# A convolution layer's Fourier transforms: the taps' spectra in a stage of their own, a fixed order on three engines, and the stream's first radix-2 stage on TensorE

## The chip, the cores and the metric

The kernel runs on one core of one Trainium2 chip. Its time is the device time of one execution, in microseconds (us). It is one launch: two state-space convolution layers and two attention layers, one after the other (called a, b, c and d here: a and c are the convolutions).

## The reference

The stream `x` has 2048 rows (time) and 640 columns (channels). Each layer is normalised, run, and added to the stream. This is the convolution layer, the only part that the change touches:

```python
P = jnp.exp(logdA[:, :, None] * l[None, None, :])
K = jnp.einsum("dn,dnl,dn->dl", Cc, P, dB).real          # 2048 taps for each of 640 channels
...
Kf = rfft2(pad(K, L))                                    # spectrum of the taps, length 4096
Uf = rfft2(pad(u^T, L))                                  # spectrum of the stream
y  = irfft2(Uf * Kf)[..., :L]^T + u * Dskip
...
x = x + _A_ref(_layernorm(x), ...)                       # layer a, and again as layer c, same taps
x = x + _B_ref(_layernorm(x), ...)                       # layers b and d: 32-head attention
```

All of it is float32. The taps are the same in layers a and c.

## The kernel before

The taps `K` are built first (`kgen`) and stored in device memory as `kd`. The convolutions then work on five chunks of 128 channels (`NCH = 5`, `DC = 128`). A transform of length 4096 is split in two: a dense part on TensorE (matrix products with a table of cosines and sines, `wf` forward, `wi` inverse, 4 MB each) and an FFT of length 8 on VectorE (`fft8`: 2 instructions of 1024 elements for each partition, 14 of 512).

For one chunk `c` of the stream:

- ScalarE writes the normalised stream to `xn`, 16 instructions of 128x128 (L615).
- `fwd`: TensorE makes four tiles `z` of 1024 columns in PSUM (L522). A `z` holds two halves, and the stage after it is a radix-2 butterfly over them: ScalarE copies one half to `zs` (L525), VectorE writes sum and difference into the spectrum `A` (L527, eight instructions of 512 elements for a chunk). Then `fft8` forward (L93 to L115).
- VectorE multiplies `A` by the spectrum of the taps `kh`, a complex product: six instructions of 2048 elements (L630 to L635). Then two more of 2048 (L636, L637), and `fft8` in the other direction, again L93 to L115.
- TensorE makes four tiles `y` with the table `wi` (L648), and VectorE adds each to the stream (L652, "the residual").

In layer a the spectrum `kh` of each chunk is made on the way, by the same `fwd` from `kd` (tiles `zk`, `Ak`; `Dskip` is added to the first tap at L601), and stored to device memory, 2 MB for a chunk (L603). Layer c loads it (L595). So layer a makes ten forward transforms and layer c five. In the last two chunks VectorE also takes the statistics for the next layer's normalisation (L557, L559), and in the last one it splits the attention's weights (L671).

The order on TensorE, VectorE and ScalarE in these layers is set by a scheduler that knows priorities and buffers, not by the source. It runs parts of one chunk's `fwd` between parts of another chunk's product and inverse.

Of the kernel before, what the change touches and what calls it, by code (L numbers as in the profile page):

```python
# [11 lines left out]
F32 = mybir.dt.float32  # L12
# [3 lines left out]
AF = mybir.ActivationFunctionType  # L16
ALU = mybir.AluOpType
# [66 lines left out]

def fft8(nc, A, B, R, sg):

    ADD, SUB = ALU.add, ALU.subtract  # L90
    plus, minus = (ADD, SUB) if sg < 0 else (SUB, ADD)
    tt, stt = nc.vector.tensor_tensor, nc.vector.scalar_tensor_tensor
    tt(B[:, 0:4], A[:, 0:4], A[:, 4:8], ADD)  # L93
# [12 lines left out]
    tt(A[:, 0:2], B[:, 0:2], B[:, 2:4], ADD)  # L106
# [5 lines left out]
    stt(A[:, 2:4], f1, RT_HALF, f0, op0=ALU.mult, op1=ADD)  # L112
    stt(A[:, 10:12], f1, -RT_HALF, f0, op0=ALU.mult, op1=ADD)
    stt(A[:, 6:16:9], f3s, sp, f2, op0=ALU.mult, op1=ADD)
    stt(A[:, 14:6:-7], f3s, sm, f2, op0=ALU.mult, op1=ADD)  # L115


class Net:
# [363 lines left out]
    def conv_setup(self, ctx):  # L482
        tc = self.tc
        if not self.wfs:
            self.conv_weights(self.nc.sync)
        self.cvp = ctx.enter_context(tc.tile_pool(name="cvp", bufs=1, reuse_waits="tile"))

        self.first = [self.new_scratch("0")]

    def conv_weights(self, eng):  # L490

# [8 lines left out]
            eng.dma_start(w[:, t].rearrange("p a b c k -> p (a b c k)"),  # L500
                          self.ins[name][:, t * 1024 : (t + 1) * 1024])

    def scratch(self, nm):
        return self.first.pop() if self.first else self.new_scratch(nm)

    def new_scratch(self, nm):
        cv = self.cvp
        return (cv.tile([P, 16, 256], F32, tag="B", bufs=1, name=f"B{nm}"),
                cv.tile([P, 8, 256], F32, tag="R", bufs=1, name=f"R{nm}"))

    def fwd(self, xn, nm):

        nc, cv = self.nc, self.cvp
        A = cv.tile([P, 16, 256], F32, tag="A", bufs=3, name=f"A{nm}")
        for t in range(4):
            z = self.ps2(f"z{nm}_{t}")
            zv = z.rearrange("p (h c k d) -> p h c k d", h=2, c=2, k=2)
            for h in (1, 0):
                for kk in range(2):
                    for c in range(2):  # L520
                        for j in range(2):
                            nc.tensor.matmul(zv[:, h, c, kk], self.wf[:, t + 4 * h, j, c, kk],  # L522
                                             xn[:, 8 * j + t + 4 * h], start=(j == 0), stop=(j == 1))
            zs = cv.tile([P, 512], F32, tag="zs", bufs=2, name=f"zs{nm}_{t}")
            nc.scalar.activation(zs, z[:, 512:1024], AF.Copy)  # L525
            for op, o in ((ALU.add, 0), (ALU.subtract, 8)):
                nc.vector.tensor_tensor(A[:, o + 2 * t : o + 2 * t + 2].rearrange("p s d -> p (s d)"),  # L527
                                        z[:, 0:512], zs, op)
        B, R = self.scratch(nm)
        fft8(nc, A, B, R, -1)  # L530
        return A

    def rows(self, dram):
# [56 lines left out]
    def kernel_spectrum(self, c, first):  # L590

        nc, cv = self.nc, self.cvp
        if not first:
            A = cv.tile([P, 16, 256], F32, tag="A", bufs=3, name=f"kh{c}")
            nc.sync.dma_start(A.rearrange("p s d -> p (s d)"), self.kh[c])  # L595
            return A
        kt = cv.tile([P, 16, DC], F32, tag="xn", bufs=3, name=f"kt{c}")
        nc.sync.dma_start(kt.rearrange("p t d -> p (t d)"), self.kd[c])
        dsk = cv.tile([1, DC], F32, tag="dsk", bufs=2, name=f"dsk{c}")
        nc.sync.dma_start(dsk, self.ins["A_Dskip"][None, c * DC : (c + 1) * DC])  # L600
        nc.vector.tensor_tensor(kt[0:1, 0, :], kt[0:1, 0, :], dsk, ALU.add)  # L601
        A = self.fwd(kt, f"k{c}")
        nc.sync.dma_start(self.kh[c], A.rearrange("p s d -> p (s d)"))  # L603
        return A

    def conv_layer(self, nm, first):
        nc, cv = self.nc, self.cvp
        rs, nmr = self.norm(nm)
        self.norm_next(nm)
        for c in range(NCH):  # L610
            x = self.x[:, :, c * DC : (c + 1) * DC]
            kh = self.kernel_spectrum(c, first)
            xn = cv.tile([P, 16, DC], F32, tag="xn", bufs=3, name=f"xn{nm}{c}")
            for t in range(16):
                nc.scalar.activation(xn[:, t], x[:, t], AF.Identity, scale=rs[:, t : t + 1],  # L615
                                     bias=nmr[:, t : t + 1])
            A = self.fwd(xn, f"{nm}{c}")
            B, T = self.scratch(f"i{nm}{c}")
            if c == 0:
                self.wi = cv.tile([P, 8, 2, 2, 2, P], F32, name="wi")  # L620
                self.load_weights(self.wi, "c_wi", nc.sync)
            if c == NCH - 1:
                self.wfs.pop().close()
                self.attn_weights()

            def m(a, c_):
                return a.rearrange("p (s c) d -> p s c d", c=2)[:, :, c_]

            tt = nc.vector.tensor_tensor
            tt(m(B, 0), m(A, 0), m(kh, 0), ALU.mult)  # L630
            tt(T, m(A, 1), m(kh, 1), ALU.mult)
            tt(m(B, 0), m(B, 0), T, ALU.subtract)
            tt(m(B, 1), m(A, 0), m(kh, 1), ALU.mult)
            tt(T, m(A, 1), m(kh, 0), ALU.mult)
            tt(m(B, 1), m(B, 1), T, ALU.add)  # L635
            tt(A[:, 0:8], B[:, 0:8], B[:, 8:16], ALU.add)  # L636
            tt(A[:, 8:16], B[:, 0:8], B[:, 8:16], ALU.subtract)  # L637
            fft8(nc, A, B, T, +1)
            v = A.rearrange("p s (k d) -> p s k d", k=2)
            for g in range(4):  # L640
                y = self.ps1(f"y{nm}{c}{g}")
                for s in range(4):
                    tau = 4 * g + s
                    t, j = tau % 8, tau // 8
                    i = 0
                    for kk in range(2):
                        for c_ in range(2):
                            nc.tensor.matmul(y[:, s * DC : (s + 1) * DC], self.wi[:, t, j, c_, kk],  # L648
                                             v[:, 2 * t + c_, kk], start=(i == 0), stop=(i == 3))
                            i += 1  # L650
                xs = x[:, 4 * g : 4 * g + 4]
                nc.vector.tensor_tensor(xs, y.rearrange("p (t d) -> p t d", t=4), xs, ALU.add)  # L652
                for tau in range(4 * g, 4 * g + 4):
                    if c >= NCH - 2:
                        self.stats_part(tau, c == NCH - 1)
                if c == NCH - 1:
                    self.norm_part(g)

    def attn_setup(self):
        dr = self.dr  # L660
# [11 lines left out]

    def attn_weights(self):

        nc, ins = self.nc, self.ins
        stack = ExitStack()
        wp = stack.enter_context(self.tc.tile_pool(name="wqp", bufs=1, side="right", reuse_waits="tile"))
        wh = wp.tile([P, 5, 692], F32R, name="wh")
        wl = wp.tile([P, 5, 692], F32R, name="wl")
# [4 lines left out]
        for k in range(5):  # L684
# [3 lines left out]
        self.split(wh[:, :, D:692], wl[:, :, D:692], kv, act=True)  # L688
        self.wqs = stack, wh, wl

    def attn_layer(self, nm, out=None):
        with ExitStack() as ctx:
# [377 lines left out]
```

## Time and profile before

| | us |
|---|---|
| median of three runs | 3169.74 (3168.94 to 3172.76) |
| the profiled execution | 3171.06 |
| its span, first to last instruction | 3169.2 |
| taps (`kgen`) | 0 to 339 |
| convolution layer a, first dense product to last residual | 352.0 to 714.8 |
| convolution layer c, the same | 1805.0 to 2079.5 |
| TensorE matmuls busy | 2787.7 (88%) |
| VectorE busy | 1375.2 (43%) |
| ScalarE busy | 2335.1 (74%) |

The span is 1.9 us shorter than the profiled execution, and that execution is 1.3 us above the median. Shares of busy time are means over four layers with different limits; the layers in question are slices 5 to 9 and 23 to 26 of the forty equal slices on the page. Neighbouring VectorE instructions overlap a little in the records: one of 512 elements is shown with 0.68 us, and the next begins 0.60 us after it began. Costs are therefore counted from start to start.

### The profile page before, as it was taken

The page shows a single profiled execution, that of the slowest core. Times are in us where ns is not written, and L with a number is a line of the kernel's source. Part 1 is how long each engine was busy: PE and PEld are TensorE (multiplying, and loading weights), DVE is VectorE, ACT ScalarE, POOL GpSimd, SP SyncE. Part 2 cuts the span into 40 slices and gives each one's busy share as a digit, 9 for nine tenths or more (in the row PEclk, how much of TensorE's full clock was granted, in tenths as well). Part 3 has the DMA queues.
Part 4 walks back from the last instruction along what each step waited for, and adds up shares of the span by engine and source line. Part 5 has one row for each costly group of instructions (what it writes and reads, how often), then busy time and mean ns, then how long its engine had stood idle before and what let it go on. Part 6 is the DMA issues. An engine that isn't in the chain of part 4 may idle for free. (4 is left out here: it accounts for less than half of the span.)

```text
span 3169.2 us, 51393 instructions
## 1 busy us (share of the span) xinstructions
PE 2787.7 (88%) x21374; PEld 1312.2 (41%) x21374; DVE 1375.2 (43%) x1699; ACT 2335.1 (74%) x2703; POOL 13.3 (0%) x60
## 2 busy tenths in 40 slices
PE   2888766749899999999999857298999999999999
PEld 0555766746422333333333557275222333333334
DVE  7888699993312212212222399943212212211222
ACT  5777312005699999999999620044999999999996
POOL 0000000000000000000000000000000000000000
PEclk9999988869999999999999978699999999999999
DMA  6011511013200000000000311023000111111111
GB/s 139 17 28 28 187 40 41 27 52 108 84 22 26 25 23 23 26 24 21 27 24 21 118 73 54 22 83 107 24 24 23 31 30 27 31 31 26 31 26 28
DMA packets 73379, 142.82 MB, mean 45 GB/s; under 512 B 22633, under 2 KB 28782, under 8 KB 70158
## 3 DMA queue, kind: packets, MB, share of 16 engines
q1 hardware_dynamic: 70018, 134.26, 14.1%
q8 instruction: 172, 2.82, 0.4%
q0 software_dynamic: 1152, 4.19, 0.3%
q10 hardware_dynamic: 1968, 0.98, 0.1%
q14 instruction: 69, 0.57, 0.1%
HBM read 82.52 MB, written 44.50 MB: 40 GB/s over the span
## 5 line engine op out<-in xcount | busy, mean ns | idle before, releaser
L880 ACT ACTIVATE pt<-scd 128x1024 f32<-128x1024 f32 x1024 | 941.5, 1200 | 8.0 <-PE scd L876 6.7
L880 ACT ACTIVATE pt<-scb 128x1024 f32<-128x1024 f32 x1024 | 941.5, 1202 | 7.5 <-PE scb L876 6.3
L890 PE MATMUL pod<-pt,vt 128*32 128x512 f32 x4096 | 547.2, 606 | 0.1
L890 PE MATMUL pob<-pt,vt 128*32 128x512 f32 x4096 | 547.2, 606 | 0.1
L876 PE MATMUL scd<-qpd,kt 62*128 62x512 f32 x2048 | 405.6, 463 | 5.4 <-DVEq L841 5.1
L876 PE MATMUL scb<-qpb,kt 62*128 62x512 f32 x2048 | 405.4, 462 | 5.3 <-DMA qpb<-mxd 5.1
L876 PEld LDWEIGHTS scb<-qpb,kt 62*128 62x128 f32 x2048 | 173.3, 184 | 433.5 <-ACT pt L880 424.0
L876 PEld LDWEIGHTS scd<-qpd,kt 62*128 62x128 f32 x2048 | 173.4, 185 | 432.4 <-ACT pt L880 422.6
L945 DVE TENSOR_TENSOR x<-pyd,x 128x320 f32<-128x320 f32 x24 | 11.8, 491 | 476.4 <-PE pyd L927 476.4
L945 DVE TENSOR_TENSOR x<-pyb,x 128x320 f32<-128x320 f32 x24 | 11.8, 491 | 476.3 <-PE pyb L927 476.3
L907 DVE RECIPROCAL rc<-rc 128x512 f32<-128x512 f32 x64 | 214.6, 3353 | 2.2
L522 PE MATMUL zc<-xnc,wf 128*128 128x128 f32 x640 | 85.3, 301 | 72.0 <-DVE Ac L527 64.5
L890 PEld LDWEIGHTS pod<-pt,vt 128*32 128x32 f32 x4096 | 80.6, 108 | 161.4 <-issue 158.6
L890 PEld LDWEIGHTS pob<-pt,vt 128*32 128x32 f32 x4096 | 80.6, 108 | 160.1 <-issue 157.2
L648 PE MATMUL ya<-Aa,wi 128*128 128x128 f32 x640 | 82.4, 297 | 69.4 <-DVE Aa L106 69.4
L393 PE MATMUL pk<-s,m 128*64 128x32 f32 x1280 | 130.8, 295 | 13.3 <-DVE s L384 13.3
L393 PE MATMUL pk<-c,e1r 128*64 128x32 f32 x1280 | 132.1, 297 | 11.4 <-DVE c L383 11.2
L393 PEld LDWEIGHTS pk<-c,e1r 128*64 128x64 f32 x1280 | 105.3, 221 | 79.6 <-issue 52.2
L904 DVE COPY on<-pod 128x512 f32<-128x512 f32 x32 | 22.1, 691 | 257.1 <-PE pod L890 254.3
L522 PE MATMUL zk<-kt,wf 128*128 128x128 f32 x640 | 83.4, 298 | 56.9 <-DVE Ak L527 43.7
L904 DVE COPY on<-pob 128x512 f32<-128x512 f32 x32 | 22.1, 691 | 239.3 <-PE pob L890 224.0
L525 ACT ACTIVATE zsc<-zc 128x512 f32<-128x512 f32 x20 | 11.9, 596 | 147.2 <-DVE Ac L527 98.3
(361 smaller groups left out, 3244.3 us busy)
## 6 DMA issues: line engine op xcount, KB each, us to landing
kh<-Ak SPq DMA_DIRECT2D x5, 2048.0 KB
qhd<-qh SPq DMA_DIRECT2D x40, 256.0 KB
qld<-ql SPq DMA_DIRECT2D x40, 256.0 KB
qpb<-qhd SPq DMA_DIRECT2D x256, 40.0 KB
kh<-kh SPq DMA_DIRECT2D x5, 2048.0 KB
qpd<-qhd SPq DMA_DIRECT2D x256, 40.0 KB
ot<-on SPq DMA_DIRECT2D x224, 40.0 KB
wi<-in_c_wi SPq DMA_DIRECT2D x16, 512.0 KB
```

What stands on the lines that cost most here:

```text
L393: nc.tensor.matmul(PK[u][64 * par : 64 * par + 64, 32 * d : 32 * d + 32], e[u][:, d, par], c[u][:, d, par], start=first, stop=not first)
L522: nc.tensor.matmul(zv[:, h, c, kk], self.wf[:, t + 4 * h, j, c, kk], xn[:, 8 * j + t + 4 * h], start=(j == 0), stop=(j == 1))
L525: nc.scalar.activation(zs, z[:, 512:1024], AF.Copy)
L648: nc.tensor.matmul(y[:, s * DC : (s + 1) * DC], self.wi[:, t, j, c_, kk], v[:, 2 * t + c_, kk], start=(i == 0), stop=(i == 3))
L876: nc.tensor.matmul(sc[:, 512 * par : 512 * par + 512], kt[rows, 128 * t : 128 * t + 128], qps[nb, hg, pr][rows], start=True, stop=True)
L880: nc.scalar.activation(pt, sc, AF.Exp, scale=SCALE)
L890: nc.tensor.matmul(po[32 * j : 32 * j + 32], vt[:, t], pts[step, j // 2][:, 512 * (j % 2) : 512 * (j % 2) + 512], start=(t == 0), stop=(t ...
L904: nc.vector.tensor_copy(on, po)
L907: nc.vector.reciprocal(rc, rc)
L945: nc.vector.tensor_tensor(xh, py, xh, ALU.add)
```

## The change

- **Kernels' spectra in a stage of their own.** Layer a begins with `kernel_spectra`: the five chunks of taps are loaded at once, by GpSimd's queue instead of SyncE's (`kts` for four chunks in the memory that the table `wi` takes later, `ktl` for the fifth in the memory of `xn`), and their five spectra are made one after the other and stored. Both layers then load `kh`, in two buffers, as layer c did.
- **A fixed order.** The whole layer runs under a manual schedule: TensorE, VectorE and ScalarE take their instructions in the order of the source. `fft8`, `product` and `radix` return lists of calls, and `weave` puts others between them.
- **First radix-2 stage on TensorE.** The taps, and the stream's chunk 0, keep the stage on VectorE (`raw`, then `radix`; ScalarE now copies the whole `z`, 1024 columns, and VectorE reads only SBUF). Chunks 1 to 4 use `dense`: each matrix product has 256 columns instead of 128, as many products as before, and sums and differences come out of the accumulation in PSUM. For it ScalarE writes half of the normalised stream twice, once negated, 24 instructions for a chunk instead of 16. ScalarE copies `z` to the spectrum (L568, 1024 elements, four for a chunk), and VectorE begins with `fft8`.
- `xn` has one buffer (three before), the spectra `A` two (three before).

On TensorE in layer a, around chunks 1 and 2 of the stream. The names: `zk2` are products for the taps of chunk 2, `za2_1` is the second `z` tile of the stream's chunk 2, `ya12` the third `y` tile of chunk 1. Before:

```order
L522 MATMUL zk2_3_3439<-kt2_3370,wf_2585 128x128 x16
L522 MATMUL za2_0_3497<-xna2_3479,wf_2585 128x128 x16
L648 MATMUL ya10_3298<-Aa1_3169,wi_2938 128x128 x4
L648 MATMUL ya11_3316<-Aa1_3169,wi_2938 128x128 x2
L648 MATMUL ya10_3298<-Aa1_3169,wi_2938 128x128 x12
L648 MATMUL ya11_3316<-Aa1_3169,wi_2938 128x128 x14
L648 MATMUL ya12_3334<-Aa1_3169,wi_2938 128x128 x16
L648 MATMUL ya13_3352<-Aa1_3169,wi_2938 128x128 x16
L522 MATMUL za2_1_3518<-xna2_3479,wf_2585 128x128 x16
```

And now:

```order
L719 MATMUL ya10_3688<-Aa1_3376,wi_3318 128x128 x16
L719 MATMUL ya11_3705<-Aa1_3376,wi_3318 128x128 x16
L719 MATMUL ya12_3728<-Aa1_3376,wi_3318 128x128 x16
L719 MATMUL ya13_3752<-Aa1_3376,wi_3318 128x128 x16
L566 MATMUL za3_0_3799<-xna3_3687,wf_2585 128x2x128 x16
L566 MATMUL za3_1_3817<-xna3_3687,wf_2585 128x2x128 x16
L566 MATMUL za3_2_3835<-xna3_3687,wf_2585 128x2x128 x16
L566 MATMUL za3_3_3853<-xna3_3687,wf_2585 128x2x128 x16
L719 MATMUL ya20_3900<-Aa2_3586,wi_3318 128x128 x16
```

The inverse products of chunk 1 are now followed by the forward products of chunk 3, two chunks ahead and twice as wide, and the taps' products have left this place.

On VectorE in layer c, between the inverse `fft8` of chunk 1 (it ends with L115, now L98) and the complex product of chunk 2. Before:

```order
L115 SCALAR_TENSOR_TENSOR Ac1_19848<-Bic1_19951 128x2x256
L527 TENSOR_TENSOR Ac2_20068<-zc2_1_20090,zsc2_1_20107 128x512 x2
L652 TENSOR_TENSOR x_66<-yc10_19977,x_66 128x4x128
L527 TENSOR_TENSOR Ac2_20068<-zc2_2_20111,zsc2_2_20128 128x512 x2
L527 TENSOR_TENSOR Ac2_20068<-zc2_3_20132,zsc2_3_20149 128x512
L652 TENSOR_TENSOR x_66<-yc11_19995,x_66 128x4x128
L527 TENSOR_TENSOR Ac2_20068<-zc2_3_20132,zsc2_3_20149 128x512
L93 TENSOR_TENSOR Bc2_20153<-Ac2_20068 128x1024
```

And now:

```order
L98 SCALAR_TENSOR_TENSOR Ac1_19704<-B_19529 128x2x256 x2
L95 TENSOR_TENSOR B_19529<-Ac2_19914 128x1024 x2
L95 TENSOR_TENSOR R_19530<-Ac2_19914 128x512 x2
L95 TENSOR_TENSOR B_19529<-R_19530 128x2x256
L726 TENSOR_TENSOR x_66<-yc10_20016,x_66 128x4x128
L95 TENSOR_TENSOR B_19529<-R_19530 128x2x256
L95 TENSOR_TENSOR B_19529<-Ac2_19914 128x2x256 x2
L95 TENSOR_TENSOR Ac2_19914<-B_19529 128x512 x2
```

The L527 rows are gone, the forward `fft8` begins right behind the inverse one, and the residuals stand inside it. In it an instruction now often reads what the one just before it wrote (`R`, then `B` from `R`), where the scheduler had put another between them.

On GpSimd's queue at the start of layer a, where before only the eight loads of `wf` stood:

```order
L519 DMA wf_2585<-in_c_wf 128x1024 x8
L642 DMA ktl_2716<-in_A_Dskip 1x16x40
L644 DMA kts_2715<-kd_68 128x2048 x4
L644 DMA ktl_2716<-kd_68 128x2048
L805 MEMSET kv_4089 128x260
```

The five loads of taps have moved here, behind the loads of the table.

The diff, cut to its core:

```diff
+def weave(calls, between):
+    for i in range(len(calls) + 1):
+        for n, call in between:
+            if n == i or (i == len(calls) and n > i):
+                call()
+        if i < len(calls):
+            calls[i]()
...
-    def fwd(self, xn, nm):
-        A = cv.tile([P, 16, 256], F32, tag="A", bufs=3, name=f"A{nm}")
+    def raw(self, xn, nm):
+        Z = self.spectrum(f"z{nm}")
...
-            zs = cv.tile([P, 512], F32, tag="zs", bufs=2, name=f"zs{nm}_{t}")
-            nc.scalar.activation(zs, z[:, 512:1024], AF.Copy)
-            for op, o in ((ALU.add, 0), (ALU.subtract, 8)):
-                nc.vector.tensor_tensor(A[:, o + 2 * t : o + 2 * t + 2].rearrange("p s d -> p (s d)"),
-                                        z[:, 0:512], zs, op)
+            nc.scalar.activation(Z[:, 4 * t : 4 * t + 4].rearrange("p s d -> p (s d)"), z, AF.Copy)
...
+    def dense(self, xn, nm):
+        A = self.spectrum(nm)
+        for t in range(4):
+            z = self.ps2(f"z{nm}_{t}")
+            zv = z.rearrange("p (c s k d) -> p s c k d", s=2, c=2, k=2)
+            for kk in range(2):
+                for c in range(2):
+                    for n, (h, j) in enumerate(((1, 0), (1, 1), (0, 0), (0, 1))):
+                        i = 4 * j + t
+                        x = (xn[:, 8 + 2 * i : 10 + 2 * i] if h
+                             else xn[:, i][:, None, :].to_broadcast([P, 2, DC]))
+                        nc.tensor.matmul(zv[:, :, c, kk], self.wf[:, t + 4 * h, j, c, kk], x,
+                                         start=(n == 0), stop=(n == 3))
+            nc.scalar.activation(A.rearrange("p (o s) d -> p o s d", o=2)[:, :, 2 * t : 2 * t + 2],
+                                 z.rearrange("p (c o e) -> p o c e", c=2, o=2), AF.Copy)
...
+    def kernel_spectra(self):
+        kts = cv.tile([P, 4, 16, DC], F32, tag="wi", name="kts")
+        ktl = cv.tile([P, 24, DC], F32, tag="xn", name="ktl")
...
+        for c in range(NCH):
+            nc.gpsimd.dma_start(ks[c].rearrange("p t d -> p (t d)"), self.kd[c])
...
+        for c in range(NCH):
+            if c + 1 < NCH:
+                skip(c + 1)
+                Z[c + 1] = self.raw(ks[c + 1], f"k{c + 1}")
+            A = cv.tile([P, 16, 256], F32, tag="kh", bufs=2, name=f"kn{c}")
+            weave(self.radix(Z.pop(c), A) + fft8(nc, A, self.B, self.R, -1), ())
+            nc.sync.dma_start(self.kh[c], A.rearrange("p s d -> p (s d)"))
...
     def conv_layer(self, nm, first):
+        with tc.manual_schedule(engines={mybir.EngineType.PE, mybir.EngineType.Activation,
+                                         mybir.EngineType.DVE}):
...
+            for c in range(NCH):
+                mul = product(A, khs.pop(c)) + fft8(nc, A, B, R, +1)
+                if c == NCH - 1:
+                    late += zip((0, 1, 3, 5, 7, 11), pieces)      # the attention weights' splits
+                weave(mul, late)
...
+                ys = [inverse(c, g, A) for g in range(2)]
+                def turn(g, c=c, A=A, ys=ys):
+                    residual(c, g, ys[g])
+                    if g < 2:
+                        ys.append(inverse(c, g + 2, A))
+                if c + 1 < NCH:
+                    weave(fft8(nc, As[c + 1], B, R, -1), [(5, lambda: turn(0)), (11, lambda: turn(1))])
+                    late = [(1, lambda turn=turn: turn(2)), (2, lambda turn=turn: turn(3))]
+                if c + 2 < NCH:
+                    for t in range(4):
+                        normals(c + 2, t)
+                    As[c + 2] = self.dense(xn, f"{nm}{c + 2}")
```

More of the change, by code (lines that the diff above doesn't have):

```diff
@@ L606, in conv_layer, with load_spectrum @@
-    def conv_layer(self, nm, first):
[L607 to L624, printed above, removed]
+    def load_spectrum(self, c):
+        A = self.cvp.tile([P, 16, 256], F32, tag="kh", bufs=2, name=f"kh{c}")
+        self.nc.sync.dma_start(A.rearrange("p s d -> p (s d)"), self.kh[c])
+        return A
@@ L626, in m @@
             def m(a, c_):
                 return a.rearrange("p (s c) d -> p s c d", c=2)[:, :, c_]
[L629 to L640, printed above, removed]
+            def product(A, kh):
+                return [lambda a=a: tt(*a) for a in (
+                    (m(B, 0), m(A, 0), m(kh, 0), ALU.mult),
+                    (R, m(A, 1), m(kh, 1), ALU.mult),
+                    (m(B, 0), m(B, 0), R, ALU.subtract),
+                    (m(B, 1), m(A, 0), m(kh, 1), ALU.mult),
+                    (R, m(A, 1), m(kh, 0), ALU.mult),
+                    (m(B, 1), m(B, 1), R, ALU.add),
+                    (A[:, 0:8], B[:, 0:8], B[:, 8:16], ALU.add),
+                    (A[:, 8:16], B[:, 0:8], B[:, 8:16], ALU.subtract))]
@@ L641, in conv_layer, with inverse @@
+            def inverse(c, g, A):
                 y = self.ps1(f"y{nm}{c}{g}")
+                v = A.rearrange("p s (k d) -> p s k d", k=2)
                 for s in range(4):
@@ L655, in conv_layer @@
                         self.stats_part(tau, c == NCH - 1)
-                if c == NCH - 1:
-                    self.norm_part(g)
+            xn = new_xn(0)
+            for t in range(4):
+                for tau in (t + 4, t + 12, t, t + 8):
+                    normal(xn[:, tau], 0, tau, rs, nmr)
+            Z = self.raw(xn, f"{nm}0")
+            As = {0: self.spectrum(f"{nm}0")}
+            khs = {c: self.load_spectrum(c) for c in range(2)}
+            self.wi = cv.tile([P, 8, 2, 2, 2, P], F32, tag="wi", name="wi")
+            self.load_weights(self.wi, "c_wi", nc.sync)
+            xn = new_xn(1)
+            for t in range(4):
+                normals(1, t)
+            weave(self.radix(Z, As[0]) + fft8(nc, As[0], B, R, -1), ())
+            As[1] = self.dense(xn, f"{nm}1")
+            pieces = []
+            late = []
+            for c in range(NCH):
+                A = As.pop(c)
+                mul = product(A, khs.pop(c)) + fft8(nc, A, B, R, +1)
+                if c == NCH - 1:
+                    late += zip((0, 1, 3, 5, 7, 11), pieces)
+                weave(mul, late)
+                late = []
+                if c + 2 < NCH:
+                    khs[c + 2] = self.load_spectrum(c + 2)
+                    xn = new_xn(c + 2)
+                ys = [inverse(c, g, A) for g in range(2)]
[6 more added lines that the diff above has]
+                    late = [(1, lambda turn=turn: turn(2)), (2, lambda turn=turn: turn(3))]
+                if c + 2 < NCH:
+                    for t in range(4):
+                        normals(c + 2, t)
+                    As[c + 2] = self.dense(xn, f"{nm}{c + 2}")
+                if c + 2 == NCH - 1:
+                    self.wfs.pop().close()
+                    pieces = self.attn_weights()
+        for g in range(4):
+            turn(g)
+            if g > 0:
+                self.norm_part(g - 1)
+        self.norm_part(3)
     def attn_setup(self):
@@ L683, in attn_weights, with piece @@
         nc.sync.dma_start(kv[:, :, 32:52], ins["B_wk"].rearrange("(k p) n -> p k n", p=P))
-        for k in range(5):
+        self.wqs = stack, wh, wl
+        def piece(k):
             wst = wp.tile([P, D], F32, tag="wst", bufs=1, name=f"wst{k}")
@@ L687, in attn_weights @@
             self.split(wh[:, k, 0:D], wl[:, k, 0:D], wst, act=True)
-        self.split(wh[:, :, D:692], wl[:, :, D:692], kv, act=True)
-        self.wqs = stack, wh, wl
+        return [lambda: self.split(wh[:, :, D:692], wl[:, :, D:692], kv, act=True)] + [
+            lambda k=k: piece(k) for k in range(5)]
     def attn_layer(self, nm, out=None):
```

89 lines of the change are left out of this document (59 added, 30 removed).

## The prediction

> **What bounds it now.** First I read the page's slices, then each layer's stretch, then what VectorE waits for, then VectorE's rows between two fixed points. Of the forty slices, of 79.2 us each, layer a is 5 to 9 and layer c 23 to 26:
>
> ```profile
> PE   2888766749899999999999857298999999999999
> DVE  7888699993312212212222399943212212211222
> PEclk9999988869999999999999978699999999999999
> ```
>
> VectorE is full there and almost idle elsewhere. The stretches give TensorE, its weight loads, VectorE, ScalarE and GpSimd (busy us, instructions), then TensorE's granted clock, the DMA share and GB/s:
>
> ```profile
> 352.00:718.00 366.00, 241.86 (x1934) 238.83 (x1935) 335.12 (x468) 56.47 (x118) 1.37 (x4) 0.83 0.15 57
> 1803.00:2083.00 280.00, 162.87 (x1297) 159.32 (x1298) 256.88 (x343) 50.46 (x115) 1.37 (x4) 0.78 0.19 72
> 430.00:450.00 20.00, 20.00 (x182) 20.00 (x181) 17.67 (x28) 1.20 (x2) 0.00 (x0) 1.00 0.26 107
> 1880.00:1900.00 20.00, 7.97 (x72) 7.77 (x70) 19.90 (x15) 1.19 (x2) 0.00 (x0) 0.81 0.20 86
> ```
>
> VectorE is busy 92% of both layers, TensorE 66 and 58%. VectorE's remaining waits, with total, count and longest:
>
> ```profile
> DVE Ac L527 <- ACT zsc L525: 17.6, 4, 12.3
> DVE Aa L527 <- ACT zsa L525: 13.2, 8, 3.1
> DVE Ak L527 <- ACT zsk L525: 11.8, 4, 6.3
> ```
>
> In layer c 12.3 of the 17.6 is the first fill; the steps have next to no idle time, so there VectorE's instructions are the time. In layer a some 3 us for each chunk are waits for ScalarE's copies. Start and duration of VectorE's rows in layer c, "x6" for six in a row:
>
> ```profile
> 1845.31 2.29 DVE L634 TENSOR_TENSOR Ric<-Ac,kh 128x2048 f32<-128x2048 f32 x1
> 1847.64 2.29 DVE L635 TENSOR_TENSOR Bic<-Bic,Ric 128x2048 f32<-128x2048 f32 x1
> ...
> 1855.45 1.21 DVE L93 TENSOR_TENSOR Bic<-Ac 128x1024 f32<-128x1024 f32 x1
> ...
> 1865.54 0.68 DVE L115 SCALAR_TENSOR_TENSOR Ac<-Bic 128x512 f32<-128x512 f32 x1
> ...
> 1912.62 0.68 DVE L115 SCALAR_TENSOR_TENSOR Ac<-Bic 128x512 f32<-128x512 f32 x1
> ...
> 1964.28 0.69 DVE L652 TENSOR_TENSOR x<-yc,x 128x512 f32<-128x512 f32 x1 [0.20 <-PE yc L648]
> ...
> 2006.76 0.68 DVE L115 SCALAR_TENSOR_TENSOR Ac<-Bic 128x512 f32<-128x512 f32 x1
> 2007.37 1.28 DVE L527 TENSOR_TENSOR Ac<-zc,zsc 128x512 f32<-128x512 f32 x2
> ...
> 2019.98 0.68 DVE L527 TENSOR_TENSOR Ac<-zc,zsc 128x512 f32<-128x512 f32 x1
> ...
> 2050.27 2.28 DVE L636 TENSOR_TENSOR Ac<-Bic 128x2048 f32<-128x2048 f32 x1
> 2052.47 2.28 DVE L637 TENSOR_TENSOR Ac<-Bic 128x2048 f32<-128x2048 f32 x1
> ...
> 2065.50 0.68 DVE L115 SCALAR_TENSOR_TENSOR Ac<-Bic 128x512 f32<-128x512 f32 x1
> ```
>
> The ends of the inverse `fft8` (start of L115 plus 0.68) mark the steps. From chunk 0 at 1866.2 to chunk 3 at 2007.4 it is 47.07 a step; the last, with the statistics and the weights' splits inside, takes 58.7. An `fft8` is 10.7 (1855.45 to 1866.18), an instruction of 2048 elements 2.20 (2050.27 to 2052.47). Layer a:
>
> ```profile
> 370.48 1.21 DVE L93 TENSOR_TENSOR B<-Ak 128x1024 f32<-128x1024 f32 x1
> 379.97 3.67 DVE L527 TENSOR_TENSOR Aa<-za,zsa 128x512 f32<-128x512 f32 x6
> ...
> 427.32 0.68 DVE L115 SCALAR_TENSOR_TENSOR Aa<-Bia 128x512 f32<-128x512 f32 x1
> ...
> 493.17 0.68 DVE L115 SCALAR_TENSOR_TENSOR Aa<-Bia 128x512 f32<-128x512 f32 x1
> ...
> 701.32 0.68 DVE L115 SCALAR_TENSOR_TENSOR Aa<-Bia 128x512 f32<-128x512 f32 x1
> ```
>
> Six of 512 elements in 3.67 makes 0.60 each, start to start. A step is 65.8 (427.3 to 493.2): a taps' chunk and a stream's chunk, and the waits.
>
> **TensorE's price.** A product in float32 is two instructions in the records.
>
> ```profile
> 352.00 16.56 PE L522 MATMUL zk<-kt,wf 128*128 128x128 f32 x128 [13.23 <-DMA kt<-kd]
> 1855.68 6.59 PE L522 MATMUL zc<-xnc,wf 128*128 128x128 f32 x32 [20.11 <-DVE Ac L527]
> 1877.08 10.88 PE L522 MATMUL zc<-xnc,wf 128*128 128x128 f32 x96
> 2062.12 16.53 PE L648 MATMUL yc<-Ac,wi 128*128 128x128 f32 x128 [43.65 <-DVE Ac L106]
> 2085.55 0.39 PE L767 MATMUL pqd<-xh,wl 128*52 128x512 f32 x1
> 2085.78 0.40 PE L767 MATMUL pqd<-xl,wh 128*52 128x512 f32 x1
> ```
>
> The full stretch above (182 in 20.00) gives 0.110 for one of 128 columns, 96 in 10.88 gives 0.113; I take 0.1115. An inverse or a `raw` chunk, 128 of them, is 14.3. `dense` has again 128, of 256 columns each. No row shows float32 in that width: the floor is no growth, 0.1115; the nearest row above is a 512-column instruction at full speed, 0.23 start to start (2085.55, 2085.78). I take 0.22, twice 0.1115, since a wider operand streams in proportion: 28.2 a chunk, bounds 14.3 and 29.6. The Trainium skill, "TensorE: Matmul & The Clock Gate", section "Wait — 56ns, not 53.3ns?", puts a product at its columns by the clock plus some 2.5 ns; twice that at 256 is an estimate of 0.218, by which the sum below would be the same.
>
> **The change, part by part.**
>
> *First radix stage on TensorE.* Each of chunks 1 to 4 loses eight L527 on VectorE, 8 x 0.60 = 4.8. `fft8` is now unmixed, so some three instructions more a step read what the one just before wrote; L635, which reads the result of L634, starts 2.33 after it instead of 2.20, so I count 0.13 for each, together 0.4. VectorE's step: 47.07 - 4.8 + 0.4, less the wait of 0.20 for TensorE at 1964.28, is 42.5. TensorE's step: 14.3 inverse + 28.2 `dense` = 42.5, without a gap if the order allows. It does: the forward products of chunk c+2 stand behind the inverse of chunk c, and VectorE needs them one whole step later. So the two engines come out equal, at 42.4 to 42.6: 4.6 off a step. ScalarE gets 24 normalisations instead of 16 and four copies of 1024 elements instead of 512:
>
> ```profile
> 1862.31 6.27 ACT L615 ACTIVATE xnc<-x,nmrc,rsc 128x128 f32<-128x128 f32 x16 [6.07 <-PE zc L522]
> L365 ACT ACTIVATE m<-pe 128x1024 f32<-128x1024 f32 x4 | 4.0, 1024 | 2.8 <-PE pe L357 2.8
> ```
>
> That is 24 x 0.39 + 4 x 1.02 = 13.5 in 42.5; the single `xn` costs nothing as long as ScalarE fills it while TensorE does the inverse, 14.3 against 9.4. Without that cover it would be up to 9 a step.
>
> *Layer c.* Three steps of 4.6 give 13.9. In the last step six L527 go (2007.37 to 2019.98), 3.6, less 0.7 for some five dependent neighbours there: 2.9. The first fill stays, 0.2 better. Together 17.
>
> *Layer a.* From its first `fft8` at 370.5 to its last inverse `fft8` at 702.0 it takes 331.5. After: the taps' first `fft8` 10.8; four more taps' chunks of 4.8 + 10.8 + 0.3 = 15.9, 63.6; chunk 0's radix and `fft8`, 15.6; its product and inverse, 8 x 2.20 + 0.4 + 10.8 = 28.8; three steps of 42.5, 127.5; the last, 58.7 - 2.9 = 55.8. Sum 302.1: 29.4 less. TensorE's 14.3 a taps' chunk lies beside VectorE's 15.9, so no wait is left; 9 to 13 of the 29.4 are today's waits for `zsk` and `zsa`. All five taps' loads come before this stage and their spectra go out during it. The reload of the first, 2 MB, is due some 80 us after its store began, and the loads of `wi` can start once the last taps in that memory have been multiplied; both lie beside VectorE's work.
>
> *Start of layer a.* The taps' loads move from SyncE's queue to GpSimd's, behind the table:
>
> ```profile
> 319.76 4.31 POOL L500 DMA_DIRECT2D wf<-in_c_wf  x8 [9.45 <-PE pe L357]
> 338.36 0.41 PE L393 MATMUL pk<-s,m 128*64 128x32 f32 x4
> 339.43 4.38 SPq L413 DMA_DIRECT2D kd<-kst  x4
> 351.96 0.28 DVE L601 TENSOR_TENSOR kt<-kt,dsk 1x128 f32<-1x128 f32 x1 [9.70 <-DMA dsk<-in_A_Dskip]
> ```
>
> Today the first product starts at 352.0, because L601 had waited 9.7 for `dsk`, not for the taps. Now one load of `Dskip` stands ahead of the taps on a queue that is otherwise idle by then, and the first chunk's taps are stored well before the last. I expect the first product near 346.5 (between 343 and 352), and the first `fft8` at 365.4 instead of 370.5: the larger copy takes back 0.4. Gain 5.1, bounds -3 to +8.
>
> *End of the layers.* The residuals behind the last inverse stay in the old form; two of the last inverse's tiles are now asked for a little later, 1 us lost at most.
>
> **The sum.** 17 + 29.4 + 5.1 - 1 = 50.5 off the profiled execution, 3171.06, which is 1.3 above the median of the runs: 3120.6, and 3119 on the median's footing. I forecast 3120. Within 0.2%, 6.3 us, a time can't be told from no change.
>
> **The rivals.**
>
> *TensorE becomes the bound.* At parity every excess counts. At 0.2315 for a wide instruction the step is 43.9, some 1.2 longer in each of six: 3128. At 0.25 it is 46.3, 3.8 longer: 3143. For it speaks that nothing on VectorE's side gives way; against, that TensorE has a store of one step built up before the first. Chance 0.20.
>
> *TensorE waits and starts slowly.* 32 instructions after 20.11 us of idle time took 6.59 instead of 3.6, 128 after 43.65 took 16.53 instead of 14.4: 2.1 to 3.0 for each long gap, and the clock is 1.00 in the full stretch but 0.81 in the one with gaps. If TensorE had such a gap in each of eight steps, 17 to 24 would come back: about 3140. The Trainium skill, "TensorE: Matmul & The Clock Gate", Part 1, says that a window of some 3.4 us without work halves the clock; the rows with their gaps of 20 and 44 us agree, and shorter ones aren't seen here. By my sum TensorE has no gap over 1 us within the steps, only ahead of a layer's first and last inverse, as today. Chance 0.05.
>
> *The taps come late, or `kh` does.* If GpSimd's loads wait for each other or for the last store, or the spectra's way through memory isn't hidden, about 10 are lost: 3130. The bandwidth in layer a, 57 GB/s on average, speaks against it. Chance 0.06.
>
> *Slower.* The operand of `dense` for one half is the same 128 columns read twice, a broadcast. If that, or float32 in 256 columns, runs at half the rate, 0.44 an instruction, a `dense` takes 56 instead of 28: 28 more in each of six steps, about 170, so 3290. The other side begins where the excess eats 50.5 in six steps, 8.4 a step, at 0.286 an instruction. No row shows a broadcast operand; every other product here runs at its columns' rate. Chance 0.05.
>
> *Better.* If VectorE's dependent neighbours cost nothing, and the taps start at 343, it is 3107 or below. Chance 0.02.
>
> **How the numbers follow.** Equal engines, as summed, have the remaining 0.62; their own range, from the bounds of the start (8 and 3 either side) and of the dependent neighbours, is 3108 to 3131. The range given reaches on into the rival of TensorE and covers late taps and most of the slow starts: 3107 to 3141. Faster by over 0.2% are all but the slower case and a remainder of mishaps together, 0.93; 0.02 within; 0.05 slower.
>
> **What the profile after would show.** The ends of the inverse `fft8` in layer c 42.4 to 42.6 apart, and the last 55.9; taps' chunks 15.9 apart in layer a; wide products 0.22 apart; TensorE's clock at 1.00 through the middle of both layers; the first taps' product at 346.5; VectorE's waits for ScalarE near nothing but for the first fill. Steps over 43.5 with VectorE waiting for copies of `z` mean TensorE's rival, or ScalarE's copies standing behind its normalisations. A wait at `kh`, at the first `z` of the taps or ahead of `wi` would make the third right. What would upset all of it is a wide product that costs more than 0.286.

## The result, and the profile after

| | before | after |
|---|---|---|
| median (runs shown beside each other) | 3170.64 us | 3116.49 us |
| lowest to highest of four | 3168.94 to 3172.76 | 3113.02 to 3118.57 |
| the profiled execution | 3171.06 | 3118.52 |

The ratio is 0.9828, with a 95% interval of 0.9811 to 0.9845: 54 us or 1.7% faster, forecast 3120 with 3107 to 3141. The same three rows of the page as before the change:

```profile
PE   2888998949899999999999899498999999999999
DVE  7888799972222122122221499932121221221222
PEclk9999999979999999999999999799999999999999
```

TensorE is now nearly full beside VectorE for most of both layers (slices 5 to 8, and 24 and 25); in slices 9 and 26, where the last step lies, it is at 4. Both layers by stretches, then 20 us out of a step of each (columns as in the prediction):

```profile
344.00:682.00 338.00, 281.38 (x1926) 264.72 (x1926) 316.76 (x430) 90.79 (x164) 1.90 (x5) 0.92 0.27 97
1768.00:2028.00 260.00, 207.64 (x1290) 191.75 (x1290) 238.57 (x310) 71.40 (x146) 1.36 (x4) 0.90 0.20 77
530.00:550.00 20.00, 20.00 (x130) 18.61 (x129) 19.93 (x21) 5.36 (x13) 0.00 (x0) 1.00 0.00 1
1880.00:1900.00 20.00, 20.00 (x108) 18.00 (x108) 19.90 (x15) 2.05 (x2) 0.00 (x0) 1.00 0.22 75
```

In a step both engines are full and the clock is 1.00. VectorE's rows: forward `fft8` of the first taps, and the last four instructions (L98) of several `fft8`. Their starts are apart by what a stage takes:

```profile
364.60 2.35 DVE L95 TENSOR_TENSOR B<-kn 128x1024 f32<-128x1024 f32 x2
...
373.01 2.50 DVE L98 SCALAR_TENSOR_TENSOR kn<-B 128x512 f32<-128x512 f32 x4
...
388.83 2.50 DVE L98 SCALAR_TENSOR_TENSOR kn<-B 128x512 f32<-128x512 f32 x4
...
480.82 2.49 DVE L98 SCALAR_TENSOR_TENSOR Aa<-B 128x512 f32<-128x512 f32 x4
...
522.97 2.49 DVE L98 SCALAR_TENSOR_TENSOR Aa<-B 128x512 f32<-128x512 f32 x4
...
663.19 2.50 DVE L98 SCALAR_TENSOR_TENSOR Aa<-B 128x512 f32<-128x512 f32 x4
...
1825.78 2.49 DVE L98 SCALAR_TENSOR_TENSOR Ac<-B 128x512 f32<-128x512 f32 x4
...
1952.24 2.50 DVE L98 SCALAR_TENSOR_TENSOR Ac<-B 128x512 f32<-128x512 f32 x4
...
2008.16 2.50 DVE L98 SCALAR_TENSOR_TENSOR Ac<-B 128x512 f32<-128x512 f32 x4
```

A taps' chunk takes 15.82 (373.01 to 388.83), a step 42.15 in both layers (480.82 to 522.97; a third of 1825.78 to 1952.24), the last 55.92. TensorE's rows in layer a show the first taps' product and two steps without a gap, a wide product 27.79 / 128 = 0.217:

```profile
344.84 60.34 PE L537 MATMUL zk<-kts,wf 128*128 128x128 f32 x512 [6.08 <-DMA kts<-kd]
...
496.25 27.79 PE L566 MATMUL za<-xna,wf 128*128 128x256 f32 x128
523.87 14.50 PE L719 MATMUL ya<-Aa,wi 128*128 128x128 f32 x128
538.21 27.79 PE L566 MATMUL za<-xna,wf 128*128 128x256 f32 x128
565.84 14.69 PE L719 MATMUL ya<-Aa,wi 128*128 128x128 f32 x128
```

Where 52.5 us between the two profiled executions went:

| stretch | before | after | change |
|---|---|---|---|
| to the first `fft8` of layer a | 370.48 | 364.60 | -5.9 |
| from there to the last inverse `fft8` of a | 331.5 | 301.1 | -30.4 |
| then to the reciprocal of c's normalisation | 1099.5 | 1100.5 | +1.1 |
| then to the end of c's first inverse `fft8` | 64.8 | 62.0 | -2.7 |
| three steps and the last one of c | 200.0 | 182.4 | -17.6 |
| the rest, attention d | 1103.0 | 1106.0 | +3.0 |

### The profile page after: what moved, and what is told of

It is laid out like the page before. It is cut to its first block, busy times and chain, and to the rows that moved or that the text cites. A ratio compares the mean times of both kernels' runs of the same rounds, so it can differ in the third digit from the quotient of the medians.

```text
span 3116.7 us, 51334 instructions
## 1 busy us (share of the span) xinstructions
PE 2874.8 (92%) x21374; PEld 1373.3 (44%) x21374; DVE 1340.8 (43%) x1639; ACT 2385.5 (77%) x2767; POOL 16.4 (1%) x66
## 5 line engine op out<-in xcount | busy, mean ns | idle before, releaser
L411 PE MATMUL pk<-c,e1r 128*64 128x32 f32 x1280 | 132.1, 297 | 11.5 <-DVE c L401 11.2
L719 PE MATMUL yc<-Ac,wi 128*128 128x128 f32 x640 | 78.5, 287 | 46.8 <-DVE Ac L95 43.7
L566 PE MATMUL za<-xna,wf 128*128 128x256 f32 x512 | 113.2, 383 | 2.7 <-ACT xna L682 2.7
L411 PEld LDWEIGHTS pk<-s,m 128*64 128x64 f32 x1280 | 108.1, 226 | 15.9 <-DVE s L402 15.9
```

What stands on the lines that cost most here:

```text
L411: nc.tensor.matmul(PK[u][64 * par : 64 * par + 64, 32 * d : 32 * d + 32], e[u][:, d, par], c[u][:, d, par], start=first, stop=not first)
L566: nc.tensor.matmul(zv[:, :, c, kk], self.wf[:, t + 4 * h, j, c, kk], x, start=(n == 0), stop=(n == 3))
```

## The experiments

The changed kernel was run in two rounds, with medians of 3116.49 and, below, 3113.48. A difference to it that is given as two numbers is taken to both. Most edits ran beside the kernel before and not beside the changed one, and the medians of the kernel before lie between 3170.64 and 3172.89, so a difference of 2 us alone settles little.

**The radix stage back on VectorE.** Order and stages stay; the products have 128 columns again and the sum and difference are made in place.

```diff
-    nc.tensor.matmul(zv[:, :, c, kk], ..., x, ...)                # 256 columns
+    nc.tensor.matmul(zv[:, h, c, kk], ..., xn[:, 8 + 2 * i if h else i], ...)
+    tt(lo, lo, hi, ALU.add)                                       # for each of four t
+    scalar_tensor_tensor(hi, hi, -2.0, lo, op0=mult, op1=add)
```

> The first radix stage of chunks 1 to 4 goes back to VectorE (eight instructions of 512 elements a chunk, in place in A), the products have 128 columns again; the fixed order and the taps' stage stay. Theory (VectorE's instructions are the time, 0.60 each): the steps between inverse fft8 ends go from 42.15 to about 46.95, the last from 55.9 to 60.7, 8 x 4.8 = 38 over the changed kernel, about 3155, still some 15 below the kernel before (the taps' stage, the earlier start, no waits for zs). Rival (the fixed order carries the gain, VectorE's instructions hide behind other work): under 3130. Rival (the fixed order by itself costs): 3170 or more.

Measured: 3153.41 (3152.31 to 3154.59) against 3172.89 of the kernel before, ratio 0.994 (0.9923 to 0.9956). Layer c's steps:

```profile
1844.77 2.50 DVE L98 SCALAR_TENSOR_TENSOR Ac<-B 128x512 f32<-128x512 f32 x4
...
1891.74 2.50 DVE L98 SCALAR_TENSOR_TENSOR Ac<-B 128x512 f32<-128x512 f32 x4
```

46.97 a step. So 37 to 40 of the gain are VectorE's 64 instructions, eight in each of eight steps, and 19.5 (14 to 24 by the interval) lie elsewhere. Of these the next sections test the queue and the order. For the taps' stage and the waits that went with it the table (above) leaves 12.8, layer a's 30.4 less the 17.6 of the same steps in layer c; no run tests it alone.

**What bounds a step?** Three kernels leave out work, on TensorE (the wide products of j = 1), on VectorE (two multiplications of the complex product in chunks 1 to 3), and both.

```diff
-    enumerate(((1, 0), (1, 1), (0, 0), (0, 1)))
+    enumerate(((1, 0), (0, 0)))                                   # first and third kernel
-    mul = product(A, khs.pop(c)) + fft8(...)
+    mul = product(A, khs.pop(c))[2 if 0 < c < NCH - 1 else 0 :] + fft8(...)   # second and third
```

> Leaves out half of the wide forward products (those of j = 1), so that a chunk has 64 wide instructions instead of 128 and TensorE's step falls from 42.1 to about 28. Theory (VectorE has no gap in the steps and is a bound by itself): steps stay at 42.15, total within 2 us of the changed kernel, about 3116. Rival (TensorE is the bound of the steps): steps fall, up to 6 x 14 us less.

> Leaves out two of the six multiplications of the complex product in chunks 1 to 3 (2 x 2.2 = 4.4 us of VectorE a step). Theory (the two engines are at parity, TensorE 14.5 + 27.7 = 42.1 to 42.2 a step without a gap): steps stay at 42.1, total 0 to 2 us less than the changed kernel, VectorE now waits for ScalarE's copies of z. Rival (VectorE alone is the bound): steps 37.75, 6 x 4.4 = 26 less, about 3090.

> Leaves out both: half of the wide products and two multiplications a step in chunks 1 to 3. Theory (parity): only together do they pay, steps 37.75, 6 x 4.4 = 26 less than the changed kernel, about 3090. Rival (something third holds the step at 42, the fixed order or the single xn): no change, 3116.

Measured: 3114.29, 3112.25 and 3086.55, the kernel before being 3172.89 (ratios 0.9821, 0.981 and 0.9729, each with an interval of 0.0016 either side). TensorE in the first, VectorE's wait in the steps of layer a in the second, then the second's VectorE in layer a, and the third's:

```profile
520.78 2.08 PE L719 MATMUL ya<-Aa,wi 128*128 128x128 f32 x8 [11.27 <-DVE Aa L95]
```

```profile
DVE B L95 <- ACT Aa L568: 9.0, 2, 4.9
```

```profile
479.76 2.50 DVE L98 SCALAR_TENSOR_TENSOR Aa<-B 128x512 f32<-128x512 f32 x4
...
517.52 2.49 DVE L98 SCALAR_TENSOR_TENSOR Aa<-B 128x512 f32<-128x512 f32 x4
...
560.31 2.50 DVE L98 SCALAR_TENSOR_TENSOR Aa<-B 128x512 f32<-128x512 f32 x4
```

```profile
481.00 2.49 DVE L98 SCALAR_TENSOR_TENSOR Aa<-B 128x512 f32<-128x512 f32 x4
...
518.75 2.50 DVE L98 SCALAR_TENSOR_TENSOR Aa<-B 128x512 f32<-128x512 f32 x4
```

With half of TensorE's wide work gone, TensorE waits 11.3 in a step and VectorE's step stays. With 4.4 of VectorE's work gone, one step shrinks to 37.8 (the spectrum of the chunk after was ready), then VectorE waits for copies of `z` and the steps are 42.8 and 41.9. The last step grows from 55.9 to 60.1, again behind copies of `z`, so that 1 to 4 us are gained of 26. With both, the steps are 37.7 and 27 to 30 come off. TensorE and VectorE bound the steps alike.

**The queue of the taps.**

```diff
-    nc.gpsimd.dma_start(ks[c]..., self.kd[c])                     # and dsk
+    nc.sync.dma_start(ks[c]..., self.kd[c])
```

> The five loads of taps and the one of Dskip go back to SyncE's queue; all else as changed. Theory (the start of layer a moved from 352.0 to 344.8 because Dskip and the taps no longer queue on SyncE): first taps' product at 351 to 353, and all of it reaches the end: 6 to 8 us more than the changed kernel, about 3123. Rival (the earlier start comes from loading all taps at once or from the single Dskip load): first product still near 345, no change, 3116.

Measured: 3122.78 (3122.34 to 3124.58). First product:

```profile
353.12 12.15 PE L537 MATMUL zk<-kts,wf 128*128 128x128 f32 x87 [13.93 <-DMA kts<-kd]
```

8.3 later than with GpSimd's queue, and 6.3 to 9.3 longer in the end: the queue accounts for the whole of the earlier start.

**The same work without the fixed order.**

```diff
-    with tc.manual_schedule(engines={PE, Activation, DVE}):
+    with ExitStack():
```

> The same work without the fixed order: TensorE, VectorE and ScalarE take the instructions as the scheduler puts them, as in the kernel before. Theory (the gain is VectorE's removed work, not the order): within 8 us of the changed kernel, 3114 to 3124, the cost being waits where wide products stand between the inverse's. Rival (at parity only a written order keeps both engines full): steps of 45 to 47 instead of 42.15, 20 to 40 more, 3136 to 3156.

Measured: 3108.96 (3107.92 to 3109.74), below the range of the first theory and 4.5 to 7.5 less than the changed kernel. In layer c's second chunk, here the scheduler's order, then the fixed one:

```profile
1858.56 1.29 DVE L95 TENSOR_TENSOR R<-Ac 128x512 f32<-128x512 f32 x2
1859.76 0.68 DVE L95 TENSOR_TENSOR B<-Ac 128x512 f32<-128x512 f32 x1
1860.36 1.28 DVE L95 TENSOR_TENSOR B<-R 128x512 f32<-128x512 f32 x2
...
1864.58 2.49 DVE L98 SCALAR_TENSOR_TENSOR Ac<-B 128x512 f32<-128x512 f32 x4
...
1906.36 2.49 DVE L98 SCALAR_TENSOR_TENSOR Ac<-B 128x512 f32<-128x512 f32 x4
```

```profile
1861.79 1.29 DVE L95 TENSOR_TENSOR R<-Ac 128x512 f32<-128x512 f32 x2
1863.12 1.29 DVE L95 TENSOR_TENSOR B<-R 128x512 f32<-128x512 f32 x2
```

An instruction that reads what its neighbour has just written begins 1.33 after the pair started, one that doesn't 1.20. The scheduler puts another between, and this step is 41.8 (1864.58 to 1906.36). In layer a, though, its first two steps are 42.8 and 43.0. From the first inverse `fft8` to the last, layer a takes 182.6 instead of 182.4 and layer c 180.8 instead of 182.4. So at parity a written order is not needed, and here it costs a little; the steps make under 2 of the 4.5 to 7.5, and where the rest comes from isn't shown.

**The splits of the weights on GpSimd.** Only the attention's weights are split so.

```diff
-    nc.vector.tensor_tensor(lo, src, hi.bitcast(F32), ALU.subtract)
+    nc.gpsimd.tensor_tensor(lo, src, hi.bitcast(F32), ALU.subtract)
```

> The subtractions in the splits of the attention's weights (five of 640 elements, 0.74 each, and one of 260, 0.33) go from VectorE to GpSimd, in both layers. Theory (VectorE alone is the time in the last step of a layer): the last steps go from 55.9 to 51.9, 8 less in all, about 3108. Rival (the slower splits come late for the attention, or GpSimd's work slows VectorE's): no change or more, 3116 to 3122.

Measured: 3108.87 (3107.32 to 3110.96), 4.6 to 7.6 less. The last step of layer a, by L98:

```profile
606.85 2.49 DVE L98 SCALAR_TENSOR_TENSOR Aa<-B 128x512 f32<-128x512 f32 x4
...
626.80 3.51 DVE L700 TENSOR_TENSOR B<-Aa,kh 128x2048 f32<-128x2048 f32 x1
...
660.70 2.49 DVE L98 SCALAR_TENSOR_TENSOR Aa<-B 128x512 f32<-128x512 f32 x4
```

53.85 instead of 55.9: of 4.0 us taken off VectorE only 2.1 came back. So the time is near the theory's and the step is not: two steps make 4.1 of the 4.6 to 7.6, and the rest isn't explained. Beside a subtraction on GpSimd (625.90 to 628.16) the first product of the step takes 3.51 instead of 2.29, and beside another one of `fft8` 1.11 instead of 0.69. These two are most of what is missing; the experiment with the residuals, below, shows the same more plainly.

**A warm clock ahead of the last inverse.**

```diff
+    late.append((8, warm))      # warm: 22 products of A[:, 15] into a PSUM tile that nobody reads
```

> Adds 22 products whose result nobody reads ahead of the last inverse of each layer, released by the eighth instruction of the last complex product. Theory (after 36 us without work TensorE's clock is half at first): the last inverse takes about 14.5 instead of 2.05 and 15.7 with a gap, the residual's wait behind the last inverse fft8 falls from 3.3 to about 1.5, 2 less in each layer, and the attention's first products find a full clock more often: 3 to 7 less than the changed kernel, 3110 to 3113. Rival (the wait comes from the order in which the tiles y are asked for, not from the clock): within 1 us of the changed kernel, or 1 to 2 more where the extra products delay the inverse.

Measured: 3112.02 (3111.75 to 3113.09), 1.5 to 4.5 less. TensorE's first row, VectorE's wait at the residuals, and the same wait and row in the changed kernel:

```profile
661.33 1.12 PE L719 MATMUL ya<-Aa,wi 128*128 128x128 f32 x8
```

```profile
DVE x L726 <- PE ya L719: 1.2, 1, 1.2
```

```profile
DVE x L726 <- PE ya L719: 3.4, 1, 3.4
```

```profile
661.62 2.05 PE L719 MATMUL ya<-Aa,wi 128*128 128x128 f32 x8 [36.44 <-DVE Aa L95]
```

Eight instructions take 1.12 instead of 2.05, and the wait is 1.2 instead of 3.4: the clock, as the theory has it, and 1 to 2 us in each layer (the two profiles of the changed kernel wait 2.4 to 3.4 there, this one 1.2).

**The changed kernel again, and three edits together** (scheduler's order, splits on GpSimd, extra products).

> The changed kernel again, word for word, beside the two below on the same chip. Its runs so far lie at 3113 to 3114 and at 3118.5. Theory (the attention of layer d finds TensorE's clock at half for its first 6 us in some executions, as in the first profile): runs in two groups some 3 to 5 us apart, and a profile in which the first products of layer d's attention are 0.23 apart belongs to the lower group. Rival (spread without such a cause): runs spread evenly over 3113 to 3119.

> Three edits together: the scheduler's order instead of the fixed one, the splits on GpSimd, the extra products ahead of the last inverse. Theory (they act in different places: 5 in starts and order, 5 to 8 in the last steps, 2 to 4 behind the last inverse): about 3100 to 3103. Rival (the scheduler's order had its gain in the last step too, so that splits and extra products add nothing to it): 3107 to 3109.

Measured: the changed kernel 3113.48 (3113.18 to 3115.05), one group, so this round doesn't show two. Its profile (3113.18) has layer d's first products 0.23 apart and takes 1102.1 for the table's last stretch, where the first profile (3118.52) has 0.43 and 1106.0; over both rounds two runs lie at 3118.5 and seven at 3113.0 to 3115.1. That fits the theory, with one profile for each group. The three edits: 3108.85 (3104.56 to 3109.23), ratio to before 0.9799 (0.9786 to 0.9812). They don't add up, and the low runs of that kernel are near the theory, the others near the rival. The half clock isn't what parts these runs: the profile of the three edits is of a low one (3105.66) and has layer d's first products 0.43 apart.

**One tile of four on VectorE again, the residuals on ScalarE and GpSimd.** On top of the three edits.

```diff
+    if t == 0: ...                # this z as in raw, copied into A; VectorE: sum and difference in place
-    tt(xs, y..., xs, ALU.add)
+    nc.scalar.activation(yb, y, AF.Copy); nc.gpsimd.tensor_tensor(xs, yb..., xs, ALU.add)   # chunks 0 to 3
```

> As the one with three edits, and one of the four tiles z of chunks 1 to 4 made as before (128 columns, radix in place on VectorE, two instructions of 0.60), while the residuals of chunks 0 to 3 go over ScalarE (a copy to SBUF) to GpSimd (the sum). Theory (parity: the step falls only when both engines are relieved): TensorE's step 42.1 - 3.4 = 38.7, VectorE's 41.9 + 1.2 - 2.4 = 40.7, the steps 40.7: some 8 less than the three edits, 3092 to 3095. Rival (GpSimd's sums come late: the y tiles in PSUM come free later and TensorE waits, or GpSimd slows VectorE): steps of 42 and more, 3100 or above.

Measured: 3142.55 (3139.88 to 3148.59), 34 more than without. GpSimd's rows, then VectorE's over the same time:

```profile
541.17 2.56 POOL L744 TENSOR_TENSOR x<-yba,x 128x512 f32<-128x512 f32 x1 [0.71 <-ACT yba L743]
544.44 2.57 POOL L744 TENSOR_TENSOR x<-yba,x 128x512 f32<-128x512 f32 x1 [0.71 <-ACT yba L743]
...
628.76 1.27 POOL L744 TENSOR_TENSOR x<-yba,x 128x512 f32<-128x512 f32 x1
```

```profile
542.53 3.35 DVE L715 TENSOR_TENSOR R<-Aa,kh 128x2048 f32<-128x2048 f32 x1
545.81 3.35 DVE L715 TENSOR_TENSOR B<-Aa,kh 128x2048 f32<-128x2048 f32 x1
```

VectorE's instructions begin 3.27 apart instead of 2.20, and GpSimd's, 1.27 while VectorE is idle, begin 3.27 apart too: the two seem to take turns, and each sum on GpSimd costs VectorE 1.07. A sum that begins beside `fft8` takes 9.91 (at 485.80), 5.90 and 7.70 in layer a's steps; meanwhile the `y` tiles in PSUM stay taken, and TensorE waits 9.3 in all for the copies of `y` and 9.9 for `fft8`. The steps of layer a are 44.7, 44.8 and 48.0 where 40.7 were expected. The Trainium skill, "SBUF — State Buffer", section "Who interferes with whom", says that a VectorE instruction with two inputs in SBUF contends with a GpSimd instruction that reads SBUF; this trace agrees, and the splits' run, with its 3.51 for 2.29, agrees too.

**A warm clock at the start of the attention too.** On the three edits, 15 more products that nobody reads, five behind each of the first three normalised rows of an attention layer.

```diff
+    if nb == 0 and i < 3:
+        for r in range(5):
+            nc.tensor.matmul(w[:, 0:P], self.ident, x[:, P * r : P * r + P], start=True, stop=True)
```

> As the version with three edits, and 15 more products that nobody reads at the start of both attention layers, five behind each of the first three normalised rows, where TensorE works about half of the time between the last inverse and the first projection. Theory (TensorE's clock drops there in some executions, as in the profile of the three edits, where 0.43 apart instead of 0.23 for 14 products costs 2.8): the first projections of layers b and d 0.23 apart, 1 us lost to the extra products, time 3104 to 3107 and less spread than 3104.6 to 3109.2. Rival (the drop comes whatever TensorE does there): 3108 to 3110, and first projections 0.43 apart in the profile.

Measured: 3104.26 (3103.45 to 3105.49), ratio to before 0.9787 (0.9773 to 0.98). First products of attention d, here and in the first profile after the change, then the stretch ahead of them in the latter and its clock:

```profile
2021.13 0.44 PE L906 MATMUL pqd<-xh,wh 128*52 128x512 f32 x1 [1.07 <-DVE xl L800]
2021.41 0.40 PE L906 MATMUL pqd<-xh,wl 128*52 128x512 f32 x1
```

```profile
2031.13 0.67 PE L894 MATMUL pqd<-xh,wh 128*52 128x512 f32 x1 [1.72 <-DVE xl L794]
2031.59 0.63 PE L894 MATMUL pqd<-xh,wl 128*52 128x512 f32 x1
```

```profile
2024.00:2031.00 7.00, 3.49 (x26) 2.54 (x25) 5.13 (x23) 5.32 (x8) 0.00 (x0) 0.95 0.00 0
2031.00:2035.00 4.00, 3.87 (x9) 1.87 (x10) 1.80 (x3) 3.44 (x5) 0.00 (x0) 0.50 0.00 0
```

From the second product on they are 0.23 apart instead of 0.43. That the extra products hold the clock isn't shown by this: of the thirteen other profiles, nine have 0.23 there without them. The time is as the theory has it, the lowest median of all versions that do the whole work, 9 to 12 less than the changed kernel, and the runs lie within 2.1 us of each other; but its interval overlaps that of the three edits (0.9786 to 0.9812).

## Why the prediction was right

Likeliest case, sign and range held; point by point:

- **Radix stage on TensorE, the steps.** Forecast 42.4 to 42.6 on both engines; measured 42.15, with no gap on either, and a wide product 0.217 where 0.22 was taken. Half of the wide products read the broadcast operand, so it costs nothing seen beyond its columns. The steps and the last step of layer c were 16.8 of the 17 forecast for it and measured 17.6. The part that was too large is that of the dependent neighbours: their price is right (0.13), but the step is only 0.1 above 47.07 - 4.82 - 0.20, not 0.4, because the order before had gaps of that size too, as the pair L634 and L635 shows: counted over a step of layer c they come to about 0.65 before and 0.78 after.
- **TensorE as the bound** (0.20) did not come, but by a margin near nothing: the experiments show that TensorE holds the step at 41.9 by itself.
- **The taps' stage.** Forecast 15.9 a chunk, 302.1 for the layer from its first `fft8`; measured 15.82 and 301.1.
- **The start.** First product forecast 346.5, measured 344.84; gain 5.1 forecast, 5.9 measured. The queue was the whole of it.
- **The first fill of layer c** was the term sized worst: 0.2 forecast, 2.7 measured. I had counted the larger copy and not the new order of ScalarE's normalisations, which now come in the order in which the first `z` needs them. Before, then after:

```profile
1802.88 8.95 ACT L615 ACTIVATE xnc<-x,nmrc,rsc 128x128 f32<-128x128 f32 x23 [1.44 <-DVE nmrc L588]
1814.39 0.60 ACT L525 ACTIVATE zsc<-zc 128x512 f32<-128x512 f32 x1 [2.56 <-PE zc L522]
```

```profile
1767.61 6.26 ACT L682 ACTIVATE xnc<-x,nmrc,rsc 128x128 f32<-128x128 f32 x16 [1.41 <-DVE rsmc L672]
1775.32 1.02 ACT L539 ACTIVATE Azc<-zc 128x1024 f32<-128x1024 f32 x1 [1.44 <-PE zc L537]
```

  From the first normalisation to the first copy it is 7.7 instead of 11.5.
- **The end of the layers.** Forecast 1 us lost, measured 4 (1.1 and 3.0 in the table). The wait at the residual in layer c grew from 2.2 to 3.3 (2.7 in the second profile), and in the profiled execution attention d began on half a clock, which costs 14 products x 0.2 = 2.8. In the second profile, with the full clock there, the two stretches together are only 0.2 longer than before. So TensorE did start slowly, but not as the rival had it: not behind a long gap in the steps but at the start of attention d, behind gaps of at most 1.72, and not in every execution.
- **Luck in the sum.** That the profiled execution came within 2.1 of the 3120.6 is in part luck: start, layer a, fill and steps came out 5.1 better than forecast, and the end 3.1 worse.
- **Slips that changed little.** A step of 43.9 is 1.4 longer than 42.5, not 1.2; the 3128 goes with 1.4. A first product between 343 and 352 gives a gain between -0.4 and 8.6, not -3 and 8. The case called better doesn't reach 3107: 3.5 at the start and 5.4 for all the neighbours counted (0.4 in seven places, 0.7 in two, 0.3 in four) make 3111.

## What to carry to other kernels

Work that moves from a full engine to a half-idle one is worth its full duration as long as the receiving engine stays below the step; add up both before and see which is the longer. At parity next to nothing that relieves one engine alone pays any more in the steps, and a written order should keep instructions that read each other's results apart. Before giving an idle GpSimd some of VectorE's sums, ask whether VectorE's instructions beside them read two operands from SBUF.

## What was not expected of the hardware

- VectorE's elementwise instructions with two inputs in SBUF and GpSimd's sums slow each other: 2.28 becomes 3.35 for the one, 1.27 becomes 2.56 for the other, and up to 9.91 for a sum beside `fft8`.
- TensorE's clock fell to 0.50 after 7 us in which it was busy for half of the time (3.49 of 7.00) and never idle for more than 1.72; in the changed kernel's second profile, with the same gaps and 3.55 of 7.00 busy, it stayed at 1.00. What decides between the two isn't shown. The Trainium skill, "TensorE: Matmul & The Clock Gate", Part 1, lets the clock fall after a window of some 3.4 us without work; this trace shows the fall without such a window.
- A float32 product of 256 columns costs 2 x 0.217, one of 128 2 x 0.113 by the rows above: 1.92 times as much for twice the columns.
